# Linear attention over 32 heads on one core: the store of head 29 split into 51, 13 and 64 partitions

## The chip, the cores and the metric

The kernel runs on one core of one Trainium2 chip. The metric is device time in microseconds (us) of one execution; several executions are made, and their median is given. Beside them one execution is recorded by the hardware profiler. Its trace gives the start and the length of every instruction, the DMA packets, and the times at which semaphores change.

## What is computed

Linear attention with the feature map elu + 1, for 32 heads of 2048 positions by 128 channels, all in bf16:

```python
phi_q = jnp.where(q > 0, q + 1, jnp.exp(q)) + 1e-6
phi_k = jnp.where(k > 0, k + 1, jnp.exp(k)) + 1e-6
kv  = jnp.einsum("bhsd,bhse->bhde", phi_k, v)
z   = jnp.einsum("bhsd->bhd", phi_k)
num = jnp.einsum("bhqd,bhde->bhqe", phi_q, kv)
den = jnp.einsum("bhqd,bhd->bhq", phi_q, z)[..., None] + 1e-6
return num / den
```

For each head, k, q and v are read (512 KB each) and the result is written (512 KB).

## The kernel before, in words

**Tiles.** One pass of the loop over h (from line 376 on) plans one head. A head's 2048 positions lie on 128 partitions of 16 positions each (`rows`, line 322), so a partition's row is 16 x 128 channels of 2 bytes, 4096 bytes in one piece in memory. k, q and v have six buffers each (NBI), the output o_sb has ten (NBO), so head 29 has output buffer 9.

**Work of a head.** ScalarE takes exp of k (L395). VectorE makes min(exp, 1) + eps of it (L401), and GpSimd the positive part of k (L398). TensorE multiplies both parts with v and with a column of ones into kvz_ps (L427, L345). It transposes q into xT_ps (L451), from which ScalarE and VectorE make the two parts of phi_q (L462, L469, L471, L483). TensorE multiplies these with kv and z into o_ps (L498, L499), and VectorE divides by the denominator into o_sb (L521 to L543). In the last two heads ScalarE takes part in the division (L551). The positive part and the other part of phi_k are added for five tiles of each head before the product (L406): by VectorE for heads 0 and 1 (all tiles of head 0, two groups of head 1), by GpSimd from head 2 on. The change leaves that as it is.

**The order.** `Plan` (lines 21 to 247) collects every operation with an engine and a key. Each engine runs its operations in the order of their keys; where an operation needs another engine's result, `emit` puts a wait for a semaphore in front of it. All loads and all stores are issued by SP (L388 and L586), in the order of their keys. A load of head h has a key near h - 7, a store has `late`, which is h + 1 + 0.18 h (line 590). So a store falls behind its head, more and more with h: the last load (head 31) has a key near 24, and the stores of the last heads are issued after all the loads, one by one, when their results are there. The store of head 29 (LAST - 2) has the key 35.22, head 30's 36.4, and the two parts of head 31's (9 tiles, then 7) 37.58 and 37.59.

**Semaphores of the stores.** Each store adds 16 to the semaphore of its buffer (`dma=("o", slot)`, line 588). Head 29's shares slot 9 with the stores of heads 9 and 19. At its end SP waits until every such semaphore has its full count:

```python
for name, n in counts.items():
    if name[0] == "o":
        eng.wait_ge(dma_sem(name), 16 * n)
```

These are lines 224 to 226, and nothing else is behind the last stores.

Of the kernel before, what the change touches and what calls it, by code (L numbers as in the profile page):

```python
# [7 lines left out]
P = 128  # L8
# [241 lines left out]
def bass_standalone__linear_attn_elu__prompt_kernel(  # L250
# [6 lines left out]
    B, H, S, D = q.shape  # L257
    assert D == P and S == 16 * P
    NT = 16
# [7 lines left out]
    NG = 7  # L267
    HALF = NT * P // 2
    LAST = NH - 1

    ADD = (1, 2, 3, 4, 5)
    SPLIT = tuple(j for j in range(NT) if j not in ADD)
# [8 lines left out]
    of = out.rearrange("b h s d -> (b h) s d")  # L281

    with ExitStack() as es:
        def sb(name, shape, dt):
            return es.enter_context(nc.sbuf_tensor(name, shape, dt))
# [13 lines left out]
        o_sb = sb("o_sb", [P, NBO, NT, D], bf16)  # L299
# [20 lines left out]
        pl = Plan()  # L320

        def rows(x, h):
            return x[h].rearrange("(p j) d -> p (j d)", j=NT)
# [42 lines left out]
        for key, n in WARM:  # L366
# [3 lines left out]
                 ("emk", 0): -2.05, ("rk", 1): -1.94, ("emq", 0): -1.93, ("zs", 0): -1.92, ("emk", 1): -1.9, ("emq", 1): -0.051,  # L370
                 ("zs", LAST): LAST - 2 + 0.957, ("kv2", LAST): LAST - 1 + 0.7015, ("kvs", LAST): LAST - 1 + 0.72}
        halves = {}
# [3 lines left out]
        for h in range(NH):  # L376
# [3 lines left out]
            bi, b2, b3, bo = h % NBI, h % 2, h % 3, h % NBO  # L380
# [107 lines left out]
            def where(g, h=h):  # L488
                if h < LAST:
                    return ofull, 512 * g, ("banko", g)  # L490
                return (xfull, 512 * g, ("bankx", g)) if g < 2 else (ofull, 512 * (g - 2), ("banko", g - 2))
# [24 lines left out]
            def res(g0, g1, where=where):  # L516
                return [where(g)[2] for g in range(g0, g1)]

            def den(g0, g1, key, h=h, b3=b3, where=where, res=res):
                full, base, _ = where(g0)  # L520
                pl.add("dve", key, lambda d: d.tensor_scalar(  # L521
                    den_sb[:, b3, 4 * g0:4 * g1].rearrange("p (a b) -> p a b", b=4),
                    _ap(full, base, [[512, g1 - g0], [NC, 4]]), EPS, None, op0=ALU.add),
                    reads=res(g0, g1), writes=[("den", b3, g) for g in range(g0, g1)])
# [12 lines left out]
            def div(g0, g1, key, h=h, bo=bo, b3=b3, rd=rd, where=where, res=res):  # L537
                full, base, _ = where(g0)
                pl.add("dve", key, lambda d: d.tensor_tensor(  # L539
                    out=o_sb[:, bo, 3 * g0:3 * g1, :].rearrange("p (a b) d -> p a b d", b=3),  # L540
                    in0=_ap(full, base + 1, [[512, g1 - g0], [NC, 3], [1, D]]),
                    in1=rd(4 * g0, [[4, g1 - g0], [1, 3], [0, D]]), op=ALU.mult),
                    reads=res(g0, g1) + [("rden", b3, g) for g in range(g0, g1)], writes=[("o", bo, g) for g in range(g0, g1)],  # L543
                       kind=("div0" if g0 == 0 else "div2") if h < LAST - 1 else "dve")

# [9 lines left out]

            if h < LAST - 1:
                den(0, NB, h + 0.9)
# [3 lines left out]
                div(2, NB, h + 0.945)  # L561
            elif h == LAST - 1:
                den(0, 2, h - 1 + 0.949)
# [18 lines left out]
                last_tile(h + 0.925)  # L582
                div(4, 5, h + 0.93)

            def store(t0, t1, key, parts, slot, h=h, bo=bo):
                pl.add("sp", key, lambda sp: sp.dma_start(rows(of, h)[:, t0 * D:t1 * D],  # L586
                                                          o_sb[:, bo, t0:t1].rearrange("p j d -> p (j d)")),
                       reads=[("o", bo, p) for p in parts], dma=("o", slot))

            late = h + 1.0 + 0.18 * h  # L590
            if h < LAST:
                store(0, NT, late, ("t", 0, 1, 2, 3, 4), bo)
            else:
                store(0, 9, late, (0, 1, 2), bo)
                store(9, NT, late + 0.01, (3, 4, "t"), NBO)
# [30 lines left out]
```

## Time and profile before

| | us |
|---|---|
| median of 3 runs | 169.86 (169.57 to 169.96) |
| the profiled execution | 169.55 |
| its span, first to last instruction | 167.8 |
| busy: PE, DVE, ACT, POOL | 158.1, 153.9, 155.7, 101.0 |
| DMA: bytes moved, mean rate | 67.25 MB, 401 GB/s |

The span is what the trace covers; the profiled execution's own time is 1.75 us longer. PE is TensorE, DVE VectorE, ACT ScalarE, POOL GpSimd; SP issues transfers. "L586" is line 586 of the kernel. A transfer is cut into packets, which 16 DMA engines move; the DMA share of a stretch is the mean busy share of these 16. A packet is counted, with its whole length and bytes, in the stretch in which it starts, which can make the share of a very short stretch wrong and over 1. "Us to landing" of a transfer is the time from its issue by SP to the last of its 16 increments of the semaphore. In a row of a table by stretch stand the stretch, its length, the busy time of PE, PEld, DVE, ACT and POOL with the number of instructions, then the granted TensorE clock, the DMA share and GB/s. In a row of waits stand the total in us, the number, and the longest.

### The profile page before, as it was taken

How to read it: one execution, taken by the hardware profiler on the slowest of the kernel's cores; microseconds unless marked ns; L12 is line 12 of the kernel's file. 1: busy time of each engine (PE TensorE's matmuls, PEld its weight loads, DVE VectorE, ACT ScalarE, POOL GpSimd, SP SyncE). 2: the span in 40 equal slices, each digit the busy share in tenths (PEclk: the TensorE clock that was granted, in tenths of full speed). 3: DMA queues.
4: the chain of work that ended last, by engine and by line, in shares of the span. 5: the costliest groups of instructions: out<-in, count | busy, mean ns of one | idle time of the engine just before them, and what ended most of it. 6: DMA issues, size and time to landing. Idle time of an engine off the chain costs nothing.

```text
span 167.8 us, 6510 instructions
## 1 busy us (share of the span) xinstructions
PE 158.1 (94%) x3143; PEld 151.4 (90%) x2449; DVE 153.9 (92%) x302; ACT 155.7 (93%) x143; POOL 101.0 (60%) x69
## 2 busy tenths in 40 slices
PE   7599999999999999999999999999999999999940
PEld 0279999999999999999999999999999999999940
DVE  0598999999999999999999999999999999999980
ACT  3979999999999999999999999999999999996880
POOL 2416677776666677766666777666667776666100
PEclk9999999999999999999999999999999999999995
DMA  5999999999999999999999999999999999999973
GB/s 192 414 421 413 417 412 415 382 395 415 412 418 414 422 417 418 421 420 415 414 421 421 414 421 418 412 420 421 418 419 418 418 418 418 421 414 416 419 321 140
DMA packets 19869, 67.25 MB, mean 401 GB/s; under 512 B 2066, under 2 KB 2194, under 8 KB 19858
## 3 DMA queue, kind: packets, MB, share of 16 engines
q1 hardware_dynamic: 19856, 67.12, 99.1%
q8 instruction: 5, 0.08, 0.2%
q14 instruction: 6, 0.05, 0.1%
q10 hardware_dynamic: 2, 0.00, 0.0%
HBM read 50.33 MB, written 16.78 MB: 400 GB/s over the span
## 4 chain that ended last, share of the span: by engine, by line
PE 84%; DVE 8%; ACT 2%; DMA 2%; issue 0%; DVEq 0%
PE kvz_ps L427 35%; PE o_ps L498 16%; PE o_ps L499 16%; PE xT_ps L451 15%; DVE o_sb L539 3%; DMA k_sb<-in_k_dram 2%; DVE rq_sb L471 1%; PE kvz_ps L345 1%; ACT ek_sb L395 1%; ACT eq_sb L462 1%; DVE emk_sb L401 1%; DVE emq_sb L483 1%; DVE rk_sb L406 1%; DVE rden_sb L527 1%; DVE den_sb L521 0%
## 5 line engine op out<-in xcount | busy, mean ns | idle before, releaser
L406 POOL TENSOR_TENSOR rk_sb<-rk_sb,emk_sb 128x640 bf16<-128x640 bf16 x30 | 41.9, 1398 | 45.9 <-DVE emq_sb L483 44.3
L427 PE MATMUL kvz_ps<-v_sb,rk_sb 128*128 128x128 bf16 (+1 forms) x512 | 68.0, 218 | 0.9 <-DVE rk_sb L406 0.9
L539 DVE TENSOR_TENSOR o_sb<-o_ps,rden_sb 128x768 bf16<-128x768 f32 (+2 forms) x62 | 67.9, 1135 | 0.0
L398 POOL TENSOR_SCALAR rk_sb<-k_sb 128x2048 bf16<-128x2048 bf16 x31 | 58.9, 1900 | 8.3 <-DMA k_sb<-in_k_dram 8.3
L462 ACT ACTIVATE eq_sb<-xT_ps 128x2048 bf16<-128x2048 bf16 (+1 forms) x33 | 60.2, 1828 | 3.9 <-PE xT_ps L451 2.8
L395 ACT ACTIVATE ek_sb<-k_sb 128x2048 bf16<-128x2048 bf16 x32 | 61.6, 1925 | 1.8 <-DMA k_sb<-in_k_dram 1.6
L499 PE MATMUL o_ps<-kvs_sb,rq_sb 128*128 128x129 bf16 (+1 forms) x536 | 61.1, 217 | 0.0
L498 PE MATMUL o_ps<-kvs_sb,emq_sb 128*128 128x129 bf16 (+1 forms) x536 | 61.1, 217 | 0.0
L345 PE MATMUL kvz_ps<-ones_sb,rk_sb 128*128 128x1 bf16 x428 | 58.5, 165 | 0.0
L427 PE MATMUL kvz_ps<-v_sb,emk_sb 128*128 128x128 bf16 (+1 forms) x334 | 53.9, 218 | 0.3 <-DVE emk_sb L401 0.2
L498 PEld LDWEIGHTS o_ps<-kvs_sb,emq_sb 128*128 128x128 bf16 x536 | 50.6, 98 | 0.0
L499 PEld LDWEIGHTS o_ps<-kvs_sb,rq_sb 128*128 128x128 bf16 x536 | 50.1, 97 | 0.0
L427 PEld LDWEIGHTS kvz_ps<-v_sb,rk_sb 128*128 128x128 bf16 x512 | 46.4, 96 | 3.1 <-DVE rk_sb L406 1.9
L345 PE MATMUL kvz_ps<-ones_sb,emk_sb 128*128 128x1 bf16 x253 | 41.5, 165 | 0.0
L451 PE MATMUL xT_ps<-ident,q_sb 128*128 128x128 bf16 x512 | 33.8, 219 | 1.0 <-DMA q_sb<-in_q_dram 1.0
L451 PEld LDWEIGHTS xT_ps<-ident,q_sb 128*128 128x128 bf16 x512 | 30.0, 98 | 4.7 <-DMA q_sb<-in_q_dram 4.3
L427 PEld LDWEIGHTS kvz_ps<-v_sb,emk_sb 128*128 128x128 bf16 x334 | 32.0, 96 | 0.7 <-DVE emk_sb L401 0.3
L469 ACT ACTIVATE rq_sb<-xT_ps 128x1024 bf16<-128x1024 bf16 x30 | 30.7, 1022 | 0.0
L401 DVE TENSOR_SCALAR emk_sb<-ek_sb 128x2048 bf16<-128x2048 bf16 x32 | 21.9, 684 | 5.2 <-ACT ek_sb L395 5.2
L471 DVE TENSOR_SCALAR rq_sb<-xT_ps 128x1024 bf16<-128x1024 bf16 x34 | 23.3, 690 | 1.0 <-PE kvz_ps L345 0.8
L483 DVE TENSOR_SCALAR emq_sb<-eq_sb 128x2048 bf16<-128x2048 bf16 x32 | 22.0, 686 | 0.0
L532 DVE TENSOR_TENSOR o_sb<-o_ps,rden_sb 128x128 bf16<-128x128 f32 x31 | 9.0, 292 | 1.1
(29 smaller groups left out, 52.1 us busy)
## 6 DMA issues: line engine op xcount, KB each, us to landing
k_sb<-in_k_dram SPq DMA_DIRECT2D x32, 512.0 KB, 14.6
q_sb<-in_q_dram SPq DMA_DIRECT2D x32, 512.0 KB, 14.1
v_sb<-in_v_dram SPq DMA_DIRECT2D x32, 512.0 KB, 14.2
out_dram<-o_sb SPq DMA_DIRECT2D x31, 512.0 KB, 14.7
out_dram<-o_sb SPq DMA_DIRECT2D x1, 288.0 KB, 4.1
out_dram<-o_sb SPq DMA_DIRECT2D x1, 224.0 KB, 4.0
first_sb<-in_v_dram ACTq DMA_DIRECT2D x1, 0.1 KB
```

The source lines that it names most:

```text
L345: return pe.add_instruction(mybir.InstMatmult(start_tensor_calc=start, stop_tensor_calc=stop, ldweights=False, bass_skip_group_check=True, ...
L395: lambda a, bi=bi, b2=b2: a.activation(ek_sb[:, b2, :], k_sb[:, bi, :], ACT.Exp),
L398: lambda e, bi=bi, b3=b3: e.tensor_scalar(rk_sb[:, b3, :], k_sb[:, bi, :], BIG, 0.0, op0=ALU.min, op1=ALU.max),
L406: pl.add(eng, key, lambda e: e.tensor_tensor(out=rk_sb[:, b3, c], in0=rk_sb[:, b3, c], in1=emk_sb[:, b3, c], op=ALU.add), reads=[("emk", b ...
L427: last = pe.matmul(kvz_ps[:, 1 - l:NC + r], lhsT=w, rhs=v_sb[:, bi, c - l:c + D + r], start=first, stop=fin, skip_group_check=True)
L451: last = pe.transpose(xT_ps[:, j * P:(j + 1) * P], q_sb[:, bi, j * P:(j + 1) * P], ident[:])
L462: halves[part] = pl.add("act", key, lambda a: a.activation(eq_sb[:, b2, c], xT_ps[:, c], ACT.Exp), reads=both[part:part + 1] or both, writ ...
L469: f = lambda a: a.activation(rq_sb[:, b3, c], xT_ps[:, c], ACT.Relu)
L471: f = lambda d: d.tensor_scalar(rq_sb[:, b3, c], xT_ps[:, c], 0.0, None, op0=ALU.max)
L498: pe.matmul(o_ap, lhsT=emq_sb[:, b3, t * P:(t + 1) * P], rhs=kvs_sb[:, b3, c0:c1], start=True, stop=False)
L499: return pe.matmul(o_ap, lhsT=rq_sb[:, b3, t * P:(t + 1) * P], rhs=kvs_sb[:, b3, c0:c1], start=False, stop=True)
L539: pl.add("dve", key, lambda d: d.tensor_tensor(out=o_sb[:, bo, 3 * g0:3 * g1, :].rearrange("p (a b) d -> p a b d", b=3), in0=_ap(full, bas ...
```

## The change

The store of one head, 29, is issued as three transfers in place of one: partitions 0 to 50, 51 to 63, and 64 to 127, all 16 tiles of each. They have the same key, so they go out one after the other in this order, and they add to the same semaphore (slot 9), whose count at the end rises from 48 to 80. All other stores keep their 128 partitions.

```diff
     LAST = NH - 1
+    PARTS = {LAST - 2: (51, 13, 64)}
...
-            def store(t0, t1, key, parts, slot, h=h, bo=bo):
-                pl.add("sp", key, lambda sp: sp.dma_start(rows(of, h)[:, t0 * D:t1 * D],
-                                                          o_sb[:, bo, t0:t1].rearrange("p j d -> p (j d)")),
+            def store(t0, t1, key, parts, slot, p0=0, p1=P, h=h, bo=bo):
+                pl.add("sp", key, lambda sp: sp.dma_start(rows(of, h)[p0:p1, t0 * D:t1 * D],
+                                                          o_sb[p0:p1, bo, t0:t1].rearrange("p j d -> p (j d)")),
                        reads=[("o", bo, p) for p in parts], dma=("o", slot))
...
             if h < LAST:
-                store(0, NT, late, ("t", 0, 1, 2, 3, 4), bo)
+                p0 = 0
+                for n in PARTS.get(h, (P,)):
+                    store(0, NT, late, ("t", 0, 1, 2, 3, 4), bo, p0, p0 + n)
+                    p0 += n
+                assert p0 == P
```

## The prediction

> **What bounds the kernel now.** I read the chain of work first, to see which engine sets the end, and then the waits of SP's queue, because the change touches only SP.
>
> ```profile
> PE 84%; DVE 8%; ACT 2%; DMA 2%; issue 0%; DVEq 0%
> ...
> SPq L220 <- ACT o_sb L551: 4.0, 2, 3.4
> SPq L226 <- DMA out_dram<-o_sb: 3.4, 2, 2.5
> ```
>
> The chain is TensorE's for 84% of the span, but it says nothing about the stores. The second row does: SP's last act is the wait of L226 for the stores' semaphores, and its longest piece is 2.5 us. So the program ends when the last store lands, after all computing. The next rows are SP's timeline, the chain's last piece, and the time to landing of the stores of heads 27, 28, 29 and 30 and of the two parts of head 31, each read in a narrow stretch around its issue.
>
> ```profile
> 157.48 0.33 SPq L586 DMA_DIRECT2D out_dram<-o_sb  x1
> 161.25 0.33 SPq L586 DMA_DIRECT2D out_dram<-o_sb  x1
> 162.64 0.33 SPq L586 DMA_DIRECT2D out_dram<-o_sb  x1
> 163.30 0.33 SPq L586 DMA_DIRECT2D out_dram<-o_sb  x1
> ...
> 162.81 0.47 DVE o_sb L539
> ...
> out_dram<-o_sb SPq DMA_DIRECT2D x1, 512.0 KB, 14.3
> ...
> out_dram<-o_sb SPq DMA_DIRECT2D x1, 512.0 KB, 10.9
> ...
> out_dram<-o_sb SPq DMA_DIRECT2D x1, 512.0 KB, 7.3
> ...
> out_dram<-o_sb SPq DMA_DIRECT2D x1, 512.0 KB, 4.8
> ...
> out_dram<-o_sb SPq DMA_DIRECT2D x1, 288.0 KB, 4.1
> out_dram<-o_sb SPq DMA_DIRECT2D x1, 224.0 KB, 4.0
> ```
>
> Head 29 (LAST - 2) is issued at 157.48 and lands at 157.48 + 7.3 = 164.8. Head 30 lands at 161.25 + 4.8 = 166.0, the parts of head 31 at 166.7 and 163.30 + 4.0 = 167.3. VectorE has finished at 163.28, so the last 4 us are transfer alone. A landing is that of the slowest of the 16 DMA engines, so the question is how many are still at work. The DMA share by stretch shows it (columns after the engines' busy times: PEclk, DMA share, GB/s).
>
> ```profile
> 160.50:161.00 0.50, 0.50 (x12) 0.50 (x10) 0.48 (x3) 0.50 (x3) 0.00 (x0) 1.00 0.77 311
> 161.00:161.50 0.50, 0.50 (x9) 0.33 (x6) 0.43 (x3) 0.36 (x2) 0.00 (x0) 1.00 0.45 180
> 161.50:162.00 0.50, 0.01 (x1) 0.00 (x0) 0.47 (x3) 0.50 (x3) 0.00 (x0) 1.00 0.36 147
> 162.00:162.50 0.50, 0.00 (x0) 0.00 (x0) 0.50 (x2) 0.48 (x3) 0.00 (x0) 1.00 0.90 369
> ...
> 164.50:165.00 0.50, 0.00 (x0) 0.00 (x0) 0.00 (x0) 0.00 (x0) 0.00 (x0) 0.50 0.78 302
> 165.00:165.50 0.50, 0.00 (x0) 0.00 (x0) 0.00 (x0) 0.00 (x0) 0.00 (x0) 0.50 0.17 68
> 165.50:166.00 0.50, 0.00 (x0) 0.00 (x0) 0.00 (x0) 0.00 (x0) 0.00 (x0) 0.50 0.07 28
> 166.00:166.50 0.50, 0.00 (x0) 0.00 (x0) 0.00 (x0) 0.00 (x0) 0.00 (x0) 0.50 0.06 24
> 166.50:167.00 0.50, 0.00 (x0) 0.00 (x0) 0.00 (x0) 0.00 (x0) 0.00 (x0) 0.50 0.04 14
> ```
>
> A share of 0.06 is one engine of 16. So from 165.5 on **one engine** works alone, until about 166.8 (0.04 of the last half microsecond is 0.64 of one engine, or 0.32 us), and its last row's landing at 167.3 ends the program. Before it, 0.17 x 16 = 2.7 engines on average between 165.0 and 165.5 say that two more end near 165.4, and the other 13 are done by 165.0. The dip at 161 tells how far ahead they are: head 30's rows come only at 162.0 (0.75 us after the issue), and in 161.5 to 162.0 just 0.36 x 16 = 5.8 engines still have rows of head 29. Some **ten engines are idle by 161.5**; three end near 162.2 and merge with head 30's start; two late ones and the latest go on without a pause. The latest needs 1.3 us for each of heads 28, 29 and 30 (163.5, 164.8, 166.0), so it is never idle.
>
> One row of data is 4096 bytes. Its time comes from the stretch 140 to 160, in which all engines are busy:
>
> ```profile
> DMA packets 2334, 8.36 MB, mean 418 GB/s; under 512 B 254, under 2 KB 254, under 8 KB 2333
> ```
>
> 418 GB/s over 16 engines is 26.1 GB/s, or 0.157 us a row; 8 rows make 1.25 us, which is the latest engine's step above. So a 128-partition store gives each engine 8 rows.
>
> **The change, part by part.** The one store becomes three, of 51, 13 and 64 partitions, the same 128 rows in all. Order, buffer and releaser stay.
>
> *The issues.* Two are added, on SP alone; ScalarE's queue issues only first_sb and POOL's nothing. The row of the line gives their bounds:
>
> ```profile
> L586 SPq DMA_DIRECT2D out_dram<-o_sb x33: 332/1042/2930, 22.0 to 163.3; - x33
> ```
>
> Two cost between 2 x 0.33 = 0.66 and 2 x 2.93 = 5.9 us. The four issues in SP's timeline above all took 0.33 with a few stores outstanding, so I take 0.66: SP is done at 158.5 in place of 157.8. Behind them stands head 30's store, which waits for ScalarE (the 3.4 us of L220) until 161.25. That wait hides them with 2.8 us to spare; without it they would delay head 30 by 0.66. At the upper bound head 30 would go out 2.4 us late. No wait is added: the three share the semaphore slot that head 29 has now, and the last wait asks for the sum.
>
> *The spread over the engines* is the heart of it. No row shows 51 or 13 partitions, but the counts of packets show that the number of engines depends on the shape:
>
> ```profile
> DMA packets 19869, 67.25 MB, mean 401 GB/s; under 512 B 2066, under 2 KB 2194, under 8 KB 19858
> ...
> q10 hardware_dynamic: 2, 0.00, 0.0%
> ...
> k_sb<-in_k_dram SPq DMA_DIRECT2D x32, 512.0 KB, 14.6
> q_sb<-in_q_dram SPq DMA_DIRECT2D x32, 512.0 KB, 14.1
> v_sb<-in_v_dram SPq DMA_DIRECT2D x32, 512.0 KB, 14.2
> out_dram<-o_sb SPq DMA_DIRECT2D x31, 512.0 KB, 14.7
> out_dram<-o_sb SPq DMA_DIRECT2D x1, 288.0 KB, 4.1
> ```
>
> With the 224 KB store SP issues 129 transfers; 129 x 16 = 2064 of the 2066 small packets are one completion per engine of each. The other two are queue 10's: first_sb, a single row, has one packet of data and one completion, so it ran on one engine. Every transfer seen gives equal shares to the engines that it uses. If that is kept for 51 rows, the number of engines must divide 51 and be at most 16: three engines with 17 rows each. 13 rows go to 13 engines, one each; 64 to all, four each. If the short transfers begin at the same engine, three engines get 17 + 1 + 4 = **22 rows, ten get 5, three get 4**, where each had 8. The other end is an even spread of all three pieces, 7 to 9 rows each. The nearest row is the one-row transfer that used one engine, so I take equal shares. The Trainium skill, "DMA: Bandwidth & Descriptors", section "Why a DMA increments its semaphore by 16 and not by 1", has it so too: the largest number up to 16 that divides the slowest dimension, on the lowest-numbered engines. By its rule the loads are the 22, 5 and 4 above; no run here shows such a shape yet.
>
> *What is late next.* The latest engine loses 3 or 4 rows: 3 x 0.157 = 0.47 or 4 x 0.157 = 0.63 us. Ten of the 13 engines outside the heavy three lose 3, so the likeliest is nearer to 0.47; I take **0.50**. Its end moves from 166.8 to 166.3. Each heavy engine gains 14 rows, 14 x 0.157 = 2.2 us. An early one, done with head 29 between 160.6 and 161.5 now, is done between 162.8 and 163.7; then come head 30 and 31, 16 rows' worth or 2.5 us, so it moves its last byte between 165.3 and 166.2, still before the latest. One that ends near 162.2 now ends at 162.2 + 2.2 + 2.5 = 166.9, level with today's end.
>
> *The completions.* The pieces have 3 + 13 + 16 = 32 completions in place of 16, at most two more on an engine. The latest engine's 1.25 to 1.3 us for 8 rows of 0.157 leaves at most 0.05 us for a transfer's own cost, so at most 0.1 us; I count 0.
>
> Sum against the profiled execution: span 167.8 - 0.50 = 167.3, its time 169.55 - 0.50 = 169.05. The median of the runs shown is 169.86, 0.31 above that execution, so the forecast is 169.86 - 0.50 = **169.36**.
>
> **The rivals.** Which engines the heavy three are, no row says; the count of early, middle, late and latest engines (10, 3, 2, 1) gives their prices.
>
> - *The heavy three hold a late engine (slower).* It ends near 165.4 now; with 2.2 us more it ends at 167.6, 0.8 us after today's 166.8: 170.66. The point from which it decides: an engine whose bytes now end later than 166.8 - 2.2 = 164.6 with no idle time at 161. For it speaks that the lag sits on single engines; nothing else.
> - *They hold the latest itself (slower).* 14 rows more: 169.86 + 2.2 = 172.1.
> - *They hold a middle engine (no change).* It ends at 166.9, so 169.86 + 0.1 at most, or 169.7 where it merges earlier.
> - *The change doesn't shift the load (no change).* With the even spread the latest engine gets 7 to 9 rows: 169.86 -+ 0.16. [...]
>
> If the heavy three were any three of 16, all would be early in 120 of 560 choices (21%), the worst a middle one in 166 (30%), a late one in 169 (30%), the latest in 105 (19%). They are not drawn at random: a transfer on few engines should take those at which the spread begins, and the engines don't begin together. Rows counted by their start in the first load:
>
> ```profile
> 1.75:1.85 0.10, 0.10 (x2) 0.00 (x0) 0.00 (x0) 0.10 (x1) 0.10 (x1) 1.00 3.35 328
> 1.85:1.95 0.10, 0.10 (x2) 0.00 (x0) 0.00 (x0) 0.10 (x1) 0.06 (x1) 1.00 0.72 82
> 1.95:2.10 0.15, 0.15 (x2) 0.00 (x0) 0.00 (x0) 0.15 (x1) 0.00 (x0) 1.00 0.21 27
> 2.10:2.20 0.10, 0.10 (x1) 0.00 (x0) 0.00 (x0) 0.10 (x1) 0.00 (x0) 1.00 0.47 123
> ```
>
> 328 GB/s x 0.10 us is 8 rows, then 2, 1 and 3: eleven engines begin by 2.1 us, the others later. Whoever is served first is ahead from the start, which puts the heavy three rather among the early ones. I roughly double the first count and take the weight from the others.
>
> **How the numbers follow.** Forecast (all three early) 0.44; middle 0.15; no shift 0.08; late 0.24; latest 0.09. About 0.2% (0.34 us) is what a measurement of this kernel can tell from no change. Faster by more than that is the forecast alone: 0.44. Within it: middle and no shift, 0.23. Slower: late and latest, 0.33. The forecast's own range is 0.47 to 0.63 off, with the spread of the runs (169.57 to 169.96) 168.95 to 169.5. The range has to hold 8 in 10, so it takes in the late case (170.66 and the same spread) and leaves the latest out: **168.9 to 170.8**.
>
> **What would show it.** In the changed profile: L586 x35 with three issues of 0.33 near 157.5 to 158.5 and head 30 still near 161.25 (issues hidden); 2066 + 16 = 2082 small packets (3 and 13 engines); a DMA share of about 3 engines (0.19) or more left between 161.5 and 162; the lone engine of the tail ending near 166.3 and the last store landing near 166.8. Wrong, if the share after 165 shows an engine at work past 166.8, if the count of small packets is 2066 + 29 = 2095 (16 engines for the 51 rows as well), or if head 30 is issued later than 161.3.

## The result and the profile after

The changed kernel takes 169.44 us (median of 22 runs, 169.12 to 170.12), the kernel before 169.80 us (22 runs, 169.57 to 170.16). The ratio is 0.9983, with a 95% interval of 0.9975 to 0.9991: faster by 0.17%, or 0.15 to 0.42 us.

The profiled execution took 169.59 us with a span of 167.8 us, as long as the one of before. It was late from its start on, ahead of anything that the change touches: ScalarE's exp for head 1 waited for its k until 9.35 us; before, it began at 8.15. These are the rows of ScalarE's timeline, of the changed kernel first, then of the kernel before.

```profile
9.35 1.91 ACT L396 ACTIVATE ek_sb<-k_sb 128x2048 bf16<-128x2048 bf16 x1 [1.23 <-DMA k_sb<-in_k_dram]
```

```profile
8.15 1.91 ACT L395 ACTIVATE ek_sb<-k_sb 128x2048 bf16<-128x2048 bf16 x1
```

In the tail the engines' work is still late by about 0.9 us, and yet the execution ends together with the earlier one. So the two profiles are compared from a point after the start: the landing of head 28's store, the last one ahead of head 29's. SP's issues of head 29's three pieces, of head 30 and of head 31's two parts, in the changed kernel (start, length):

```profile
158.36 0.33 SPq L587 DMA_DIRECT2D out_dram<-o_sb  x1
158.74 0.32 SPq L587 DMA_DIRECT2D out_dram<-o_sb  x1
159.09 0.94 SPq L587 DMA_DIRECT2D out_dram<-o_sb  x1
162.13 0.36 SPq L587 DMA_DIRECT2D out_dram<-o_sb  x1
163.52 0.35 SPq L587 DMA_DIRECT2D out_dram<-o_sb  x1
164.18 0.33 SPq L587 DMA_DIRECT2D out_dram<-o_sb  x1
```

SP's waits from 155 on, in the same kernel (total, times, longest):

```profile
SPq L220 <- ACT o_sb L552: 2.6, 2, 2.0
SPq L226 <- DMA out_dram<-o_sb: 2.5, 1, 2.5
```

The three issues are over at 160.0, and SP then still waits 2.0 us for ScalarE before head 30: the added issues are hidden. The last wait is again the one for the stores. The counts of packets, and the times to landing of head 28's store (issued at 153.54) and of the last one:

```profile
DMA packets 19885, 67.25 MB, mean 401 GB/s; under 512 B 2082, under 2 KB 2210, under 8 KB 19874
...
out_dram<-o_sb SPq DMA_DIRECT2D x1, 512.0 KB, 10.4
...
out_dram<-o_sb SPq DMA_DIRECT2D x1, 224.0 KB, 3.1
```

2082 is 2066 - 16 + 3 + 13 + 16: the pieces ran on 3, 13 and 16 engines. Head 28 landed at 153.54 + 10.4 = 163.94 and the last store at 164.18 + 3.1 = 167.28, **3.34 us** apart. Before, it was 152.66 + 10.9 = 163.56 to 163.30 + 4.0 = 167.30, **3.74 us**. By these rows 0.40 us are gained from there to the end, but they give times to landing to 0.1 us only. The semaphore records of the two traces are finer: head 28 and the last store land at 163.99 and 167.30 after the change, 3.30 us apart, and at 163.52 and 167.28 before it, 3.76 us apart. So the gain is **0.46 us**, against 3 rows x 0.157 = 0.47. The tail of the changed kernel by stretch (DMA share and GB/s are the last columns):

```profile
161.00:161.50 0.50, 0.50 (x14) 0.50 (x12) 0.50 (x1) 0.50 (x4) 0.00 (x0) 1.00 0.91 238
161.50:162.00 0.50, 0.50 (x12) 0.50 (x10) 0.45 (x4) 0.50 (x3) 0.00 (x0) 1.00 0.98 270
...
165.50:166.00 0.50, 0.00 (x0) 0.00 (x0) 0.00 (x0) 0.00 (x0) 0.00 (x0) 0.50 0.73 281
166.00:166.50 0.50, 0.00 (x0) 0.00 (x0) 0.00 (x0) 0.00 (x0) 0.00 (x0) 0.50 0.28 106
166.50:167.00 0.50, 0.00 (x0) 0.00 (x0) 0.00 (x0) 0.00 (x0) 0.00 (x0) 0.50 0.10 36
```

Two things differ from before. The lone engine of the tail has company: 0.28 x 16 = 4.5 engines between 166.0 and 166.5, where there was one. In the last stretch 0.10 x 16 x 0.5 = 0.8 us of engine time are left, where 0.04 gave 0.3 us before. The packets that start between 166.8 and 166.9, of the changed kernel first, then of the kernel before, are completions alone:

```profile
DMA packets 2, 0.00 MB, mean 0 GB/s; under 512 B 2, under 2 KB 2, under 8 KB 2
```

```profile
DMA packets 1, 0.00 MB, mean 0 GB/s; under 512 B 1, under 2 KB 1, under 8 KB 1
```

Two engines end the changed kernel together, where one did before.

And the dip at 161 is gone, but not because more is moved: a share of 0.91 at 238 GB/s means 0.91 x 16 x 4096 B / 238 GB/s = 0.25 us for a row. Before, in the same stretch, 0.45 and 180 GB/s give 0.16 us. Some rows are slow; a mean over 16 engines doesn't say whose.

### The profile page after: what moved, and what is told of

It reads as the page before. It is cut to its first block, busy times and chain, and to the rows that moved or that the text cites. A ratio compares the mean times of both kernels' runs of the same rounds, so it can differ in the third digit from the quotient of the medians.

```text
span 167.8 us, 6512 instructions
## 1 busy us (share of the span) xinstructions
PE 158.3 (94%) x3143; PEld 151.3 (90%) x2449; DVE 154.2 (92%) x302; ACT 156.0 (93%) x143; POOL 100.8 (60%) x69
## 2 busy tenths in 40 slices
DMA packets 19885, 67.25 MB, mean 401 GB/s; under 512 B 2082, under 2 KB 2210, under 8 KB 19874
## 4 chain that ended last, share of the span: by engine, by line
PE 85%; DVE 5%; DMA 4%; ACT 1%; SPq 1%; issue 0%; DVEq 0%
PE kvz_ps L428 35%; PE o_ps L499 17%; PE o_ps L500 16%; PE xT_ps L452 15%; DMA k_sb<-in_k_dram 4%; DVE o_sb L540 3%; PE kvz_ps L346 1%; ACT ek_sb L396 1%; SPq L389 1%; DVE rden_sb L528 1%; DVE rq_sb L472 0%; DVE emq_sb L484 0%; DVE den_sb L522 0%; DVE emk_sb L402 0%; DVE o_sb L533 0%
```

## The experiments

The theory: the engine that is behind all others sets the end, and what counts is how many of head 29's rows it gets. The rivals: the pieces themselves bring the gain, whoever carries the rows; or another engine takes over as the last. Most edits below replace the change's one line; times are medians, with the ratio to the kernel before measured beside it.

**Pieces without a shift.**

```diff
-    PARTS = {LAST - 2: (51, 13, 64)}
+    PARTS = {LAST - 2: (64, 64)}
```

> Head 29's store as 64 and 64 partitions. Theory (the latest engine is relieved of rows): every engine keeps 4 + 4 = 8 rows, nobody is relieved, so 169.8 within 0.2. Rival (the pieces or their extra issues bring the gain, not the shift): about 169.4, as with 51, 13 and 64. Both: 2066 + 16 = 2082 small packets. If rows from one half of the partitions are slow, the rows of the early engines take about 0.25 to 0.3 us near 161 in place of 0.157; the latest engine, which gets there alone, keeps about 0.16.

Measured: 169.6 us, ratio 0.9985 (0.9971 to 1.0), 2082 small packets.

```diff
-    PARTS = {LAST - 2: (51, 13, 64)}
+    PARTS = {LAST - 2: (0, 1)}
...
-                p0 = 0
-                for n in PARTS.get(h, (P,)):
-                    store(0, NT, late, ("t", 0, 1, 2, 3, 4), bo, p0, p0 + n)
-                    p0 += n
-                assert p0 == P
+                for p0 in PARTS.get(h, (0,)):
+                    store(0, NT, late, ("t", 0, 1, 2, 3, 4), bo, p0, 2 if h in PARTS else 1)
```

`store` takes the rows p0:P:st of both sides here, in o_sb and in memory, st being its last argument.

> Head 29's store as the 64 even and the 64 odd partitions. Theory: again 8 rows for each engine, 169.8 within 0.2. On the slow rows seen near 161 in the changed kernel: if they come from pieces that lie in one part of the partitions, rows here take 0.157 us; if any store of fewer than 128 partitions has slow rows, they take 0.25 to 0.3 us here too.

Measured: 169.65 us, 0.9993 (0.9982 to 1.0004). Both agree with the theory within its 0.2 us, and the times alone don't exclude for 64, 64 that pieces bring 0.1 to 0.2 us. Their tails do more: from head 28's landing to the last one both need 3.74 us, as before. The slow rows show a difference. The stretch 160.5 to 161 of 64, 64 first, then 161 to 161.5 of even and odd:

```profile
160.50:161.00 0.50, 0.50 (x13) 0.50 (x11) 0.50 (x1) 0.50 (x4) 0.00 (x0) 1.00 1.06 385
```

```profile
161.00:161.50 0.50, 0.50 (x11) 0.44 (x8) 0.43 (x3) 0.35 (x3) 0.00 (x0) 1.00 0.51 205
```

1.06 and 385 GB/s are 0.18 us a row, 0.51 and 205 are 0.16: with halves some rows are a little slow, with even and odd partitions none.

**Leaving engines out at the top end.**

```diff
-    PARTS = {LAST - 2: (51, 13, 64)}
+    PARTS = {LAST - 2: (120, 8)}
```

> Head 29's store as 120 and 8 partitions: by equal shares 15 engines get 8 rows, eight of them one more, and one engine gets none. Theory: if the engine left out is the latest, its end moves by 8 x 0.157 = 1.25 us, to 168.6 or as far as the two next late ones allow (they ended 1.4 us before it); if it is another one, no gain: 169.8 to 170.0. Rival (the pieces themselves bring the gain): 169.4.

Measured: 169.98 us, 1.0012 (0.9999 to 1.0025).

```diff
-    PARTS = {LAST - 2: (51, 13, 64)}
+    PARTS = {LAST - 2: (104, 24)}
```

> Head 29's store as 104 and 24 partitions: by equal shares 13 engines get 8 rows, twelve of them two more, and three engines get none. Theory: if the latest is one of the three left out, 168.6 to 169.0; if not, up to two rows more on it, 169.8 to 170.1. Rival (the pieces themselves bring the gain): 169.4.

Measured: 170.02 us, 1.0014 (1.0002 to 1.0025). Neither relieves the latest engine; both are on the side of a row or two more. The rival's 169.4 is out. The counts of the two profiles:

```profile
DMA packets 19876, 67.25 MB, mean 400 GB/s; under 512 B 2073, under 2 KB 2201, under 8 KB 19865
```

```profile
DMA packets 19878, 67.25 MB, mean 400 GB/s; under 512 B 2075, under 2 KB 2203, under 8 KB 19867
```

2066 - 16 + 15 + 8 = 2073 and 2066 - 16 + 13 + 12 = 2075: the largest divisor up to 16 again.

**Loading the first seven, six and five engines.**

```diff
-    PARTS = {LAST - 2: (51, 13, 64)}
+    PARTS = {LAST - 2: (119, 9)}
```

> Head 29's store as 119 and 9 partitions: seven engines with 17 rows, nine with one more. From 51, 13, 64 (5 rows on the latest engine) and 120, 8 (9 rows on it) the latest is one of the 4th to the 8th. Theory: if it is the 8th, it keeps 1 row and its end moves by 7 x 0.157 = 1.1 us; seven engines get 18 rows, 1.6 us more, and stay in front of it unless they are late ones: 168.7 to 169.0. If it is the 4th to the 7th, it gets 10 rows more: 171.4. Rival (which engine is relieved does not matter): 169.4.

Measured: 171.52 us, 1.0116 (1.0073 to 1.0158).

```diff
-    PARTS = {LAST - 2: (51, 13, 64)}
+    PARTS = {LAST - 2: (49, 49, 30)}
```

> Head 29's store as 49, 49 and 30 partitions: seven engines with 7 + 7 + 2 = 16 rows, eight with 2, one with none. Theory: if the latest is the 8th engine, it keeps 2 rows, 6 x 0.157 = 0.94 us less, and the seven get 1.26 us more: 168.8 to 169.1. If it is the 4th to the 7th: 171.0. Rival (only the idle time near 161 counts, not who is relieved): 169.4.

Measured: 171.11 us, 1.0065 (1.0039 to 1.009).

```diff
-    PARTS = {LAST - 2: (51, 13, 64)}
+    PARTS = {LAST - 2: (102, 26)}
```

> Head 29's store as 102 and 26 partitions: six engines with 17 + 2 = 19 rows, seven with 2, three with none. Theory: if the latest is at place 7 it keeps 2 rows, 0.94 us less: 168.9; at place 4 to 6 it gets 19 rows, 1.7 us more: 171.5.

Measured: 171.63 us, 1.0102 (1.0066 to 1.0138).

```diff
-    PARTS = {LAST - 2: (51, 13, 64)}
+    PARTS = {LAST - 2: (25, 25, 25, 25, 28)}
```

> Head 29's store as four times 25 and 28 partitions: five engines with 4 x 5 + 2 = 22 rows, nine with 2, two with none. Theory: at place 6 or 7 the latest keeps 2 rows, 168.9, if none of the heavy five is a late one; at place 4 or 5 it gets 22 rows, 2.2 us more: 172.0.

Measured: 172.18 us, 1.0118 (1.0075 to 1.016). All four are on the branch in which the latest engine is among the loaded ones: it is at place 5 or earlier. The tail of 119, 9 shows one engine alone, until about 168.9 where before it was 166.8. Of these 2 us 0.3 lie ahead of head 28's landing, and 1.6 are the 10 rows more:

```profile
167.00:167.50 0.50, 0.00 (x0) 0.00 (x0) 0.00 (x0) 0.00 (x0) 0.00 (x0) 0.50 0.06 25
167.50:168.00 0.50, 0.00 (x0) 0.00 (x0) 0.00 (x0) 0.00 (x0) 0.00 (x0) 0.50 0.06 23
168.00:168.50 0.50, 0.00 (x0) 0.00 (x0) 0.00 (x0) 0.00 (x0) 0.00 (x0) 0.50 0.06 25
168.50:169.00 0.50, 0.00 (x0) 0.00 (x0) 0.00 (x0) 0.00 (x0) 0.00 (x0) 0.50 0.05 18
```

**Loading the first four.**

```diff
-    PARTS = {LAST - 2: (51, 13, 64)}
+    PARTS = {LAST - 2: (68, 60)}
```

> Head 29's store as 68 and 60 partitions: four engines with 17 + 4 = 21 rows, eleven with 4, one with none. 119, 9 and 49, 49, 30 put the latest engine at place 4 to 7. Theory: at place 5 to 7 it keeps 4 rows, 0.63 us less, 169.2; at place 4 it gets 21 rows, 13 more or 2.0 us, 171.8. Rival (the size of the gain does not follow the rows of the latest engine): 169.4 to 169.8.

Measured: 170.02 us, 1.0009 (0.999 to 1.0029). Neither branch: with 21 rows the latest would have given 171.8, with 4 rows and nobody else in the way 169.2. Its tail is 3.94 us, longer than the change's 3.34, so one of the four loaded engines ended last. It is most simply the fourth, since the first three carry even 22 rows in the change and are done earlier there. The latest is not the fourth, then, and not one of the first three, which the change loads and still gains. With place 5 or earlier from the runs above it is the **fifth**. By the prediction's sums a late engine with 13 rows more would end 0.6 us after the former end (165.4 + 2.0 against 166.8) and a middle one 0.1 ahead of it (162.2 + 2.0 + 2.5). The tail is 0.2 us longer than before, so which of the two the fourth is isn't shown.

**Overloading the first three, and another head.**

```diff
-    PARTS = {LAST - 2: (51, 13, 64)}
+    PARTS = {LAST - 2: (51, 51, 26)}
```

> Head 29's store as 51, 51 and 26 partitions: three engines with 17 + 17 + 2 = 36 rows, ten with 2, three with none. Theory: the latest keeps 2 rows and ends 0.94 us sooner, but the three heavy engines get 28 rows or 4.4 us more and become the last: bytes to 167.5 to 168.4 in place of 166.8, so 170.5 to 171.4, more if their rows are slow. Rival (only the latest engine's rows count): 168.9.

Measured: 171.5 us, 1.0086 (1.0052 to 1.0121). The latest has 2 rows here, and the end is still 1.7 us later: the heavy engines have become the last, the second limit. This run also shows slow rows in another place:

```profile
161.00:161.50 0.50, 0.50 (x9) 0.32 (x6) 0.43 (x3) 0.36 (x2) 0.00 (x0) 1.00 0.31 123
161.50:162.00 0.50, 0.00 (x0) 0.00 (x0) 0.47 (x3) 0.50 (x3) 0.00 (x0) 1.00 0.30 123
162.00:162.50 0.50, 0.00 (x0) 0.00 (x0) 0.50 (x2) 0.48 (x3) 0.00 (x0) 1.00 0.52 139
...
161.24 0.36 SPq L587 DMA_DIRECT2D out_dram<-o_sb  x1
```

From 161 to 162 five engines are at work, and the three with 36 rows must be among them; a row takes 0.16 us (0.30 and 123 GB/s). So pieces of 51 partitions on three engines are not slow by themselves. Head 30's store, a whole one, is issued at 161.24, and its rows bring in the idle engines at 162: now 0.52 and 139 GB/s are 0.25 us a row. So the rows of a whole store can be slow too.

```diff
-    PARTS = {LAST - 2: (51, 13, 64)}
+    PARTS = {LAST - 7: (51, 13, 64)}
```

> 51, 13 and 64 on head 24's store in place of head 29's. Theory: the latest engine is never idle, so 3 rows fewer bring the same 0.47 us wherever they are left out: 169.3 to 169.5, like the change. Rival (the slow rows of such pieces, 0.25 us and more while all engines are at work, delay the latest too, and the gain needs the idle time near 161): 169.8 or later.

Measured: 169.39 us, 0.9981 (0.9957 to 1.0004). The median is the theory's, but the interval reaches to no change. The profile, of an execution of 169.82 us, shows no gain: by the semaphore records 10.59 us lie between head 23's landing and the last one, where before there were 10.56 and in the changed kernel 10.18. So it isn't shown that rows left out at another head bring the same.

**The same shares from spread partitions.**

```diff
-    PARTS = {LAST - 2: (51, 13, 64)}
+    PARTS = {LAST - 2: ((0, 102, 2), (102, P, 2), (1, P, 2))}
...
-                p0 = 0
-                for n in PARTS.get(h, (P,)):
-                    store(0, NT, late, ("t", 0, 1, 2, 3, 4), bo, p0, p0 + n)
-                    p0 += n
-                assert p0 == P
+                for p0, p1, st in PARTS.get(h, ((0, P, 1),)):
+                    store(0, NT, late, ("t", 0, 1, 2, 3, 4), bo, p0, p1, st)
```

Here `store` takes the rows p0:p1:st.

> Head 29's store again as 51, 13 and 64 rows, but the first two pieces from the even partitions and the 64 from the odd ones, so that each piece reaches over all the partitions. The shares of the engines stay 22, 5 and 4 (2082 small packets) and the latest keeps 5 rows. Theory: 169.3 to 169.4 like the change, because the latest engine sets the end; the rows near 161 take nearer to 0.16 us than to 0.25 and the three heavy engines are done sooner. Rival (the slow rows of the pieces eat part of the gain of the change): 0.1 to 0.2 us less than the change, 169.2, and without the change's runs near 169.8.

Measured: 170.58 us, 1.004 (1.0023 to 1.0057). Both expectations fail. SP's issues of the three pieces took up to 1.65 us, and the rows were no faster:

```profile
157.95 0.89 SPq L587 DMA_DIRECT2D out_dram<-o_sb  x1
158.90 0.87 SPq L587 DMA_DIRECT2D out_dram<-o_sb  x1
159.80 1.65 SPq L587 DMA_DIRECT2D out_dram<-o_sb  x1
```

```profile
161.00:161.50 0.50, 0.50 (x13) 0.50 (x11) 0.47 (x3) 0.50 (x3) 0.00 (x0) 1.00 0.49 123
161.50:162.00 0.50, 0.48 (x9) 0.30 (x6) 0.44 (x2) 0.34 (x2) 0.00 (x0) 1.00 0.54 147
...
167.00:167.50 0.50, 0.00 (x0) 0.00 (x0) 0.00 (x0) 0.00 (x0) 0.00 (x0) 0.84 0.06 25
167.50:168.00 0.50, 0.00 (x0) 0.00 (x0) 0.00 (x0) 0.00 (x0) 0.00 (x0) 0.50 0.05 18
```

0.49 and 123 GB/s are 0.26 us a row with half of the engines at work. The latest has 5 rows as in the change, but the tail is 4.34 us in place of 3.34: another engine ended last, most likely a heavy one, as with 51, 51, 26. That the slow rows come only from pieces that lie in one part of the partitions doesn't fit this run, but it changes the step between the rows and SP's issues as well.

**The rows of the latest engine against the tail.** Taking the fifth place, the shares give its rows in every kernel. The tail is the time from head 28's landing to the last landing in each profile; forecast is 3.74 + 0.157 for each row above 8. The tails are made of times to landing that are printed to 0.1 us.

| pieces | rows on the 5th | tail, us | forecast |
|---|---|---|---|
| 128 (before) | 8 | 3.74 | |
| 51, 13, 64 | 5 | 3.34 | 3.27 |
| 64, 64; even and odd | 8 | 3.74; 3.74 | 3.74 |
| 120, 8 | 9 | 3.94 | 3.90 |
| 104, 24 | 10 | 4.04 | 4.05 |
| 49, 49, 30 | 16 | 5.03 | 5.00 |
| 119, 9 | 18 | 5.34 | 5.31 |
| 102, 26 | 19 | 5.54 | 5.47 |
| four times 25, 28 | 22 | 5.94 | 5.94 |
| 68, 60 | 4 | 3.94 | 3.11 |
| 51, 51, 26 | 2 | 5.63 | 2.80 |
| 51, 13, 64 spread | 5 | 4.34 | 3.27 |

In the first nine lines the fifth engine's rows give the tail within 0.1 us, and within 0.06 us if the finer semaphore records are used. In the last three lines the tail is 0.8 us or more longer than these rows ask for, so another engine is last. This table is what carries the cause.

## Why the prediction was right

*What bounds the kernel*: right. One engine, never idle, ends the program; ten kernels' tails follow its rows.

*The issues, 0.66 us hidden behind ScalarE's wait*: hidden, though the third took 0.94 us and all three 1.67.

*The shares 22, 5 and 4*: right; 2082 small packets, and the counts of the other kernels follow the same rule. The Trainium skill's rule of the largest divisor up to 16 ("DMA: Bandwidth & Descriptors", section "Why a DMA increments its semaphore by 16 and not by 1") is borne out. That the short transfers begin at the same engine is borne out by the table.

*The latest loses 3 rows, 0.47 us, taken as 0.50*: right. By the semaphore records the tail is 0.46 us shorter, with nothing for the completions, as forecast. The medians gain less, 0.36 with 0.15 to 0.42. Why they do stays open. Two things are on record. The heavy engines are the next limit, and closer than forecast: their bytes were to be done by 166.2 at the latest, 0.1 us or more ahead of the latest engine, or by 166.7 in this profile, in which head 28 lands 0.5 us later. In it the last two completions start together after 166.8, one of the latest engine and the other most likely of a heavy one, so an execution in which a heavy engine is a little later gains less. The sum for these engines took 0.157 us for each of their 14 extra rows; some rows near 161 took more, but whether theirs did isn't shown. Also, 9 of the 22 runs lie between 169.59 and 170.12, the other 13 between 169.12 and 169.45. The profiled one is of the first group, with its late start; whether all nine start late isn't known, because they have no profile.

*The heavy three are early engines*: right by the outcome, with a chance of 0.44, so there was luck in it. The reason given was that the engines served first are ahead from the start. No run tells which engines begin first, and the runs put the latest engine only two places behind the last of the heavy three. Of the counts tried from the first place on, three gains, four (170.02) gains nothing, and five (172.18) loses. The profile of before could not tell that.

*The signs*: one that was named as a sign of being wrong came up, since head 30 was issued at 162.13 and not by 161.3. The issues did not cause it, because SP still waited 2.0 us for ScalarE; this execution was late as a whole. For the same reason its last byte and last landing stand at 166.8 and 167.3, where they stood before, and not 0.5 us earlier.

*The rivals*: the Trainium skill advises against two transfers of disjoint partition halves ("DMA: Bandwidth & Descriptors", section "Rules for kernel authors"). The trace agrees for the halves: 64, 64 left the tail at 3.74 us. Even and odd partitions, which shift nothing either, left it there too. Unequal shares are another case, in which the engine that ends last is relieved.

## What to carry to other kernels

When the last wait is for a store, look at the DMA share after the last instruction: a share near 1/16 means that one engine is behind, and that bytes on the other 15 cost nothing until they reach it. The number of partitions of a transfer chooses its engines (51 means three), so it can move rows between them; which engine is behind has to be measured, by loading the first three, five, seven engines in turn, because a wrong guess costs six times what a right one brings (2.3 us up from 169.88 to 172.18 against 0.36 down from 169.80 to 169.44). The gain ends where the loaded engines become the last, and with 22 rows on three engines that limit was already close.

## What the runs showed of the hardware

- Rows of 4096 bytes can be slow: as a mean over the engines at work 0.25 us near 161 with 51, 13, 64, 0.26 with the same shares from even and odd partitions, 0.25 in head 30's whole store behind 51, 51, 26, 0.18 with 64, 64 (and 0.20 from 159.5 to 160, at 1.06 and 344 GB/s), and 0.16 with even and odd halves and in the kernel before. The Trainium skill ("SBUF — State Buffer", section "Door 1: The DMA port swizzle") has partitions 0 to 63 reach only 8 of the 16 ports, and 64 to 127 the other 8. 64, 64 against even and odd agrees with that; the spread pieces with 0.26 us and the whole store with 0.25 don't. The cause stays open.
- The issue of a piece that steps over every second partition took SP 0.87 to 1.65 us with the shares 22, 5 and 4, where the change's took 0.32 to 0.94. Stepping alone is not the reason: the even and odd halves took 0.54 and 0.60 us, and 64, 64 took 0.55 and 0.60. The reason is open too.
- In all profiles the latest of the 16 engines fits one place, the fifth, counted from the engine at which the short transfers begin. What delays it was not tried.
